# A deeper ring of exponential tiles, an earlier turn for the last shifted curves, and smaller filler matmuls in a multi-query attention kernel

## The chip, the cores and the metric

The kernel runs on one core of a Trainium2 chip. The metric is the device time of one execution in microseconds (us). A profiled execution has a span, from its first to its last instruction, that is about 2 us shorter than its device time (773.3 against 775.11 us for the kernel before). PE is TensorE, ACT is ScalarE, DVE is VectorE.

## The reference

The program takes x of 2048 rows by 512 in bf16 and returns `x + s * g`.

```python
xn = layernorm(x)
q  = (xn @ wq)            # 32 heads of 16
k  = xn @ wk              # one key head, 16 wide, shared by all heads
v  = xn @ wv              # one value head
p  = softmax(q k^T / 4)   # 32 heads x 2048 x 2048
s  = (p v) @ wo
g  = silu(silu(xn @ w1) @ w2)     # 1792 wide inside
return x + s * g
```

The work is 32 x 2048 x 2048 exponentials. The kernel cuts them into 2048 *score tiles* of 128 keys by 512 queries; 64 of them form a *group*, and there are 32 groups.

## The kernel before

The kernel is a list scheduler that runs when the program is built. It keeps a clock for every engine, knows an estimated duration of each operation, and writes down a fixed order of instructions for each engine. So a change of one of its constants changes the order of thousands of instructions; on the chip only the semaphores decide when each starts.

A score tile can go two ways. On ACT, two or three tiles that lie side by side in PSUM go through one exponential into a slot of the ring `pa_sb`. On DVE, one instruction turns a tile into a first curve (`db_sb`, a bf16 exponential built by integer arithmetic), and four tiles share four instructions that make *shifted curves* from it (`ds_sb`), whose weighted sum approximates the exponential. Either way PE then multiplies the curves by the values ("PV") and accumulates into one PSUM bank. That bank must be transposed out by DVE before the next group's PV may begin.

```python
NPA, NDB, NDS = 6, 4, 2 * (K - 1)          # six slots of exponentials
pa_sb = sb("pa_sb", [P, NPA, 3 * NQ], BF16)

def pv_round(t):                            # which PV matmuls can go now?
    # ... cut: nothing before the last group's bank is transposed
    if len(got) < 4 and nleft[g] > 0 and t - old < HOLD and a_pressure() < NPA - 2 and pe_share(t) > LOW_USE:
        return ("wait", min(soon, old + HOLD))
    return ("go", got)

def act_step():                             # ACT takes an exponential only with a free slot
    # ... cut
    free = [k for k in range(NPA) if pa_busy[k] == 0]
    if free:
        s = min(free, key=lambda k: pl.ready(AC, (), [("pA", k)]))
        rx = pl.ready(AC, [("ps", b) for b in u.banks[:len(u.slots)]], [("pA", s)])

# DVE: shifted curves have priority 6, evacuations of score tiles 0 or 2
pl.add(Task(DV, T_SH, lambda v, s=s, j=j, bb=bt.b: v.tensor_scalar(
    ds_sb[:, s, :], db_sb[:, bb, :], SHIFT[j], None, op0=ALU.add),
    [("Db", bt.b, i) for i in range(4)], ds_keys(s), 6, list(bt.P.values()), on_place=placed))

# a filler: four matmuls on zeros, when PE was busy less than LOW_USE of the last 3 us
elif st["assigned"] > 0 and not tail["made"]:
    fb = fill_bank(t)
```

The softmax here doesn't subtract the row's maximum and nothing guards it: scores larger than these inputs give would overflow.

## Time and profile before

The median is 773.68 us of 4 runs (772.73 to 774.03).

These are lines of the profile's page of the kernel before: busy time of each engine with its share of the span, the chain of waits by engine and by line, and the three costliest groups of ACT and DVE (after the bar: busy us, mean ns of one, then idle time just before them and what ended it).

```profile
PE 704.9 (91%) x8640; PEld 202.7 (26%) x8640; DVE 738.3 (95%) x1290; ACT 747.4 (97%) x758; POOL 19.9 (3%) x46
...
ACT 88%; DVE 6%; PE 5%; DMA 1%; issue 0%; SPq 0%; ACTq 0%; DVEq 0%
...
L1200 ACT ACTIVATE pa_sb<-ps 128x1024 bf16<-128x1024 f32 (+1 forms) x679 | 734.0, 1377 | 8.3 <-PE ps L695 4.7
L871 DVE TENSOR_SCALAR db_sb<-ps 128x512 uint16<-128x512 f32 x492 | 328.5, 686 | 13.8 <-PE ps L695 11.8
L905 DVE TENSOR_SCALAR ds_sb<-db_sb 128x2048 uint16<-128x2048 uint16 x492 | 323.6, 684 | 1.0
```

ACT is the bound: 88% of the chain, with 679 exponentials of 2 or 3 tiles. DVE makes 492 of the 2048 tiles. Mean durations overlap from one instruction to the next; in the chain of waits five exponentials in a row, three of two tiles and two of three (from 75.80 us), take 5.44 us. That is 12 tiles, so ACT needs about 0.453 us a tile.

The next answer cuts the span of the kernel before at the first exponential (13.62 us), at 22 us and at the end of the last exponential (763.83 us). Columns: stretch, its length, then busy us (and instructions) of PE, weight loads, DVE, ACT, POOL, the granted PE clock, the DMA share and GB/s.

```profile
core 0: us, PE busy (x) PEld busy (x) DVE busy (x) ACT busy (x) POOL busy (x), PEclk, DMA share, GB/s
0.00:13.62 13.62, 9.75 (x91) 4.22 (x92) 10.27 (x30) 3.94 (x7) 7.36 (x17) 1.00 0.86 280
13.62:22.00 8.38, 7.73 (x73) 3.40 (x71) 6.56 (x21) 6.18 (x5) 4.45 (x9) 0.59 1.08 375
22.00:763.83 741.83, 683.54 (x8416) 193.13 (x8414) 715.54 (x1229) 737.32 (x746) 8.14 (x20) 1.00 0.02 7
763.83:773.30 9.47, 3.85 (x66) 1.90 (x66) 5.93 (x12) 0.00 (x1) 0.00 (x0) 0.96 0.16 57
```

ACT idles 2.2 us in the head (8.38 less 6.18), while the clock of PE is granted at 0.59 on average, and 4.5 us in the body. The list of waits of the kernel before (us in total, times, longest) says for what, from 40 us on:

```profile
ACT pa_sb L1200 <- PE ps L965: 3.1, 3, 1.4
ACT pa_sb L1200 <- PE ps L695: 0.8, 1, 0.8
```

Line 965 is the PV matmul. An exponential reads scores, not PV, so a wait for PV is a wait for a free slot of the ring. The timeline of the kernel before shows the last of the three (start, duration, idle before it in brackets):

```profile
722.47 0.71 DVE L982 STREAM_TRANSPOSE f_sb<-ps 128x512 f32<-128x512 f32 x1
...
723.66 0.59 PE L965 MATMUL ps<-pa_sb,v_sb 128*32 128x512 bf16 x5
...
724.09 1.45 ACT L1200 ACTIVATE pa_sb<-ps 128x1536 bf16<-128x1536 f32 x1 [1.30 <-PE ps L965]
```

DVE transposes the output bank of a closing group at 722.47 us. Only then can PE consume exponentials of the next group (723.66 us), which empties a slot; ACT has stood for 1.30 us. DVE itself waits for score matmuls, 28 times from 40 to 757 us:

```profile
DVE db_sb L871 <- PE ps L695: 10.4, 28, 0.8
```

### The profile page before, as it was taken

To read this page: it belongs to the slowest core of one execution; us is meant where nothing else is said; L and a number is where in the kernel's file an instruction comes from. 1 tells how busy PE (TensorE), PEld (TensorE's weight loads), DVE (VectorE), ACT (ScalarE), POOL (GpSimd) and SP (SyncE) were. 2 spreads that over 40 slices of the span, in tenths; PEclk is the share of its full clock that TensorE was granted. 3 is DMA by queue.
4 is the path that set the end of the run, shared out by engine and by line. 5 is a ranking of instruction groups with operands and counts; after the bars stand their busy time and mean duration, and the time that the engine had idled before them with its cause. 6 is when DMAs were issued, how large, how long until landed. Compare 5 with 4: busy or idle time off the path is not lost.

```text
span 773.3 us, 19855 instructions
## 1 busy us (share of the span) xinstructions
PE 704.9 (91%) x8640; PEld 202.7 (26%) x8640; DVE 738.3 (95%) x1290; ACT 747.4 (97%) x758; POOL 19.9 (3%) x46
## 2 busy tenths in 40 slices
PE   7999899999989999999988999999998999999985
PEld 3322222222222222222222222222222222222221
DVE  8699999999999998999999999999999999999994
ACT  4999999999999999999999999999999999999995
POOL 5400000000000000000000000000000000000000
PEclk8999999999999999999999999999999999999999
DMA  9300000000000000000000100000000000000000
GB/s 311 85 3 2 2 1 2 2 2 2 1 2 16 29 14 2 2 2 1 2 2 2 29 28 2 2 1 2 3 2 1 15 16 29 2 3 1 2 2 28
DMA packets 11429, 12.57 MB, mean 16 GB/s; under 512 B 1808, under 2 KB 10768, under 8 KB 11344
## 3 DMA queue, kind: packets, MB, share of 16 engines
q1 hardware_dynamic: 10288, 11.28, 4.5%
q8 instruction: 69, 1.13, 0.6%
q10 hardware_dynamic: 1056, 0.03, 0.1%
q14 instruction: 16, 0.13, 0.1%
HBM read 8.95 MB, written 2.10 MB: 14 GB/s over the span
## 4 chain that ended last, share of the span: by engine, by line
ACT 88%; DVE 6%; PE 5%; DMA 1%; issue 0%; SPq 0%; ACTq 0%; DVEq 0%
ACT pa_sb L1200 83%; ACT t_sb L523 3%; DVE db_sb L871 2%; DVE ds_sb L905 2%; PE ps L965 1%; PE ps L695 1%; PE ps L396 1%; ACT t_sb L546 1%; DMA ds_sb<-in_A_x_dram 1%; DVE stats_sb L357 1%; PE ps L438 0%; SPq L315 0%; PE ps L412 0%; DVE f_sb L982 0%; DVE qt_sb L503 0%
## 5 line engine op out<-in xcount | busy, mean ns | idle before, releaser
L1200 ACT ACTIVATE pa_sb<-ps 128x1024 bf16<-128x1024 f32 (+1 forms) x679 | 734.0, 1377 | 8.3 <-PE ps L695 4.7
L871 DVE TENSOR_SCALAR db_sb<-ps 128x512 uint16<-128x512 f32 x492 | 328.5, 686 | 13.8 <-PE ps L695 11.8
L905 DVE TENSOR_SCALAR ds_sb<-db_sb 128x2048 uint16<-128x2048 uint16 x492 | 323.6, 684 | 1.0
L695 PE MATMUL ps<-qt_sb,kt_sb 32*128 32x512 bf16 x2048 | 267.7, 385 | 51.9 <-ACT pa_sb L1200 41.1
L965 PE MATMUL ps<-ds_sb,v_sb 128*32 128x512 bf16 x1968 | 258.5, 384 | 2.3 <-DVE ds_sb L905 1.7
L965 PE MATMUL ps<-pa_sb,v_sb 128*32 128x512 bf16 x1556 | 245.7, 386 | 2.3 <-DVE ds_sb L905 1.5
L695 PEld LDWEIGHTS ps<-qt_sb,kt_sb 32*128 32x128 bf16 x2048 | 68.5, 91 | 333.6 <-ACT pa_sb L1200 273.3
L965 PE MATMUL ps<-db_sb,v_sb 128*32 128x512 bf16 x492 | 132.5, 387 | 3.0 <-DVE f_sb L982 2.8
L965 PEld LDWEIGHTS ps<-ds_sb,v_sb 128*32 128x32 bf16 x1968 | 65.8, 95 | 63.5 <-issue 28.3
L965 PEld LDWEIGHTS ps<-pa_sb,v_sb 128*32 128x32 bf16 x1556 | 61.3, 95 | 55.5 <-issue 34.9
L396 PE MATMUL ps<-w_sb,u_sb 128*32 128x512 bf16 x896 | 75.1, 384 | 0.0
L396 PE MATMUL ps<-xnT_sb,w_sb 128*32 128x512 bf16 x896 | 72.5, 384 | 0.7 <-DVE db_sb L871 0.4
L523 ACT ACTIVATE t_sb<-ps 128x512 bf16<-128x512 f32 x56 | 47.5, 848 | 0.0
L965 PEld LDWEIGHTS ps<-db_sb,v_sb 128*32 128x32 bf16 x492 | 33.0, 95 | 21.8 <-issue 9.1
L525 DVE SCALAR_TENSOR_TENSOR u_sb<-t_sb,ps 128x512 bf16<-128x512 bf16 x56 | 38.2, 682 | 0.3 <-ACT t_sb L523 0.2
L982 DVE STREAM_TRANSPOSE f_sb<-ps 128x512 f32<-128x512 f32 x32 | 22.8, 712 | 7.4 <-PE ps L965 7.4
L396 PEld LDWEIGHTS ps<-w_sb,u_sb 128*32 128x32 bf16 x896 | 18.8, 94 | 29.9 <-issue 24.2
L396 PEld LDWEIGHTS ps<-xnT_sb,w_sb 128*32 128x32 bf16 x896 | 18.5, 94 | 29.5 <-issue 18.6
L396 PE MATMUL ps<-xnT_sb,wq_sb 128*32 128x512 bf16 x256 | 20.3, 383 | 0.0
L396 PE MATMUL ps<-wo_sb,on_sb 128*32 128x512 bf16 x256 | 19.9, 383 | 0.0
L986 DVE TENSOR_TENSOR otr_sb<-f_sb,rcp_sb 128x256 bf16<-128x256 f32 x32 | 13.3, 416 | 0.0
L546 ACT ACTIVATE t_sb<-ps 128x512 bf16<-128x512 f32 x16 | 13.0, 815 | 0.0
(44 smaller groups left out, 161.0 us busy)
## 6 DMA issues: line engine op xcount, KB each, us to landing
w_sb<-in_B_w_dram SPq DMA_DIRECT2D x2, 1792.0 KB, 13.2
xr_sb<-in_A_x_dram SPq DMA_DIRECT2D x16, 128.0 KB, 2.2
out_dram<-ob_sb SPq DMA_DIRECT2D x16, 128.0 KB, 1.7
ds_sb<-in_A_x_dram SPq DMA_DIRECT2D x3, 512.0 KB, 7.7
ds_sb<-in_A_x_dram SPq DMA_DIRECT2D x4, 128.0 KB, 2.6
wq_sb<-in_A_wq_dram SPq DMA_DIRECT2D x1, 512.0 KB, 5.4
wo_sb<-in_A_wo_dram SPq DMA_DIRECT2D x1, 512.0 KB, 14.6
kt_sb<-kt_sb SPq DMA_DIRECT2D x4, 64.0 KB, 2.3
```

What stands on the lines that cost most here:

```text
L357: ts_ = pl.add(Task(DV, 593.0, lambda v, t=t: v.bn_stats(stats_sb[:, t, :], x_tile(t)), [xkey(t)], [("st", t)], 1 + j, gate=(lambda: q_don ...
L396: last = h.matmul(bank(b)[32 * j:32 * (j + 1), :], lhsT=lhs(j), rhs=rhs, start=start, stop=stop, tile_position=(0, 32 * j), skip_group_che ...
L523: t1 = Task(AC, 477.0, lambda a: a.activation(t_sb[:, k, :], bank(b), ACT.Tanh, scale=0.5), [("ps", b)], [("t", k)], 0)
L525: t2 = Task(DV, T_P, lambda v: v.scalar_tensor_tensor(out=u_sb[:, ft, :], in0=t_sb[:, k, :], scalar=1.0, in1=bank(b), op0=ALU.add, op1=ALU ...
L546: t1 = Task(AC, 477.0, lambda a: a.activation(t_sb[:, k, :], bank(b), ACT.Tanh, scale=0.25), [("ps", b)], [("t", k)], 0)
L695: return pe.matmul(bank(b), lhsT=kt_sb[32 * i:32 * i + 32, g % 2, kt * P:(kt + 1) * P], rhs=qt_sb[32 * i:32 * i + 32, (g // 2) % NQR, :], ...
L871: bt.P[i] = pl.add(Task(DV, T_P, lambda v, b=b, i=i, bb=bt.b: v.tensor_scalar(db_sb[:, bb, i * NQ:(i + 1) * NQ], bank(b), 128.0 * LOG2E, 1 ...
L905: pl.add(Task(DV, T_SH, lambda v, s=s, j=j, bb=bt.b: v.tensor_scalar(ds_sb[:, s, :], db_sb[:, bb, :], SHIFT[j], None, op0=ALU.add), [("Db" ...
L965: h = pe.matmul(bank(OB)[32 * i:32 * (i + 1), :], lhsT=lhs, rhs=rhs, start=s0, stop=s1, tile_position=(0, 32 * i), skip_group_check=True)
L982: t1 = pl.add(Task(DV, T_TR, lambda v: v.transpose(f_sb[:, k, :], bank(OB)), [("ps", OB)], [("F", k)], 1, [norm.get(("m", g - 2))]))
L986: t3 = pl.add(Task(DV, 332.0, lambda v: v.tensor_tensor(o3[:, :, val:val + DH], f3[:, :, val:val + DH], rcp_sb[:, k, :].unsqueeze(2).to_br ...
L1200: op = pl.place(AC, 0.8333 * NQ * n + T_AF, lambda a: a.activation(pa_sb[:, s, 0:n * NQ], ps[:, b0 * 512:(b0 + n) * 512], ACT.Exp), [("ps" ...
```

## The change

Its intent: let ACT run ahead over the close of a group, close groups sooner, and keep PE's clock up with fillers that cost less.

```diff
-LOW_USE, USE_WIN = 0.5, 3000.0
+LOW_USE, HIGH_USE, USE_WIN = 0.55, 0.8, 3000.0
+CLOSING, URGENT = 3, 1.5
+NPA, PRESS = 9, 4
@@ pv_round and pe_step: the pressure threshold stays at four
-... a_pressure() < NPA - 2 and pe_share(t) > LOW_USE:
+... a_pressure() < PRESS and pe_share(t) > LOW_USE:
@@ shifted curves
-    ..., 6, list(bt.P.values()), on_place=placed))
+    ..., lambda g=bt.g: URGENT if g == st["gO"] and nleft[g] <= CLOSING else 6, list(bt.P.values()), on_place=placed))
@@ fillers
-if "zer" not in pl.lastw or pe_share(t) > LOW_USE:
+if "zer" not in pl.lastw or pe_share(t) > (LOW_USE if t > 30000.0 else HIGH_USE):
@@ do_fill: 256 columns instead of 512; one 128x128 matmul where PE is in that mode
-elif st["assigned"] > 0 and not tail["made"]:
+elif t_done and not tail["made"]:
     fb = fill_bank(t)
@@ cut: filler durations, warm-up condition
```

More of the change, by code (lines that the diff above doesn't have):

```diff
@@ L160, in best @@
             if r <= t + 25.0:
-                key = (task.prio, k)
+                key = (task.prio() if callable(task.prio) else task.prio, k)
                 if now is None or key < now[0]:
@@ L257, in bass_recurrent_scan__grouped_kv_mqa__dense_activation_silu__prompt_kernel @@
     POOL_BANKS = (5, 7)
-    NPA, NDB, NDS = 6, 4, 2 * (K - 1)
+    NDB, NDS = 4, 2 * (K - 1)
     NQR, NON = 4, 2 * NOC
@@ L392, in job, with col4 @@
             return jb
-        def col4(h, b, lhs, rhs, start, stop):
+        def col4(h, b, lhs, rhs, start, stop, n=NQ):
             for j in range(4):
-                last = h.matmul(bank(b)[32 * j:32 * (j + 1), :], lhsT=lhs(j), rhs=rhs, start=start, stop=stop,
+                last = h.matmul(bank(b)[32 * j:32 * (j + 1), 0:n], lhsT=lhs(j), rhs=rhs, start=start, stop=stop,
                                 tile_position=(0, 32 * j), skip_group_check=True)
@@ L906, in make_shifts @@
                         ds_sb[:, s, :], db_sb[:, bb, :], SHIFT[j], None, op0=ALU.add),
-                        [("Db", bt.b, i) for i in range(4)], ds_keys(s), 6, list(bt.P.values()), on_place=placed))
+                        [("Db", bt.b, i) for i in range(4)], ds_keys(s),
+                                lambda g=bt.g: URGENT if g == st["gO"] and nleft[g] <= CLOSING else 6, list(bt.P.values()), on_place=placed))
         x_free = [False]
@@ L938, in pv_round @@
                 return ("wait", soon)
-            if len(got) < 4 and nleft[g] > 0 and t - old < HOLD and a_pressure() < NPA - 2 and pe_share(t) > LOW_USE:
+            if len(got) < 4 and nleft[g] > 0 and t - old < HOLD and a_pressure() < PRESS and pe_share(t) > LOW_USE:
                 return ("wait", min(soon, old + HOLD))
@@ L1118, in do_fill @@
         def do_fill(t, b):
-            pl.place(PE, MM, lambda pe: col4(pe, b, lambda j: zer_sb[:, 32 * j:32 * (j + 1)], zer_sb[:, :], True, True),
-                     ["zer"], [("ps", b)], t0=pe_start(t, "C"))
-            pl.mode = "C"
+            mode = pl.mode if pl.mode in ("C", "F") else "C"
+            if mode == "C":
+                emit = lambda pe: col4(pe, b, lambda j: zer_sb[:, 32 * j:32 * (j + 1)], zer_sb[:, 0:NQ // 2], True, True, NQ // 2)
+            else:
+                emit = lambda pe: pe.matmul(bank(b)[:, 0:NQ // 2], lhsT=zer_sb[:, 0:P], rhs=zer_sb[:, 0:NQ // 2], start=True, stop=True)
+            pl.place(PE, MM / 2, emit, ["zer"], [("ps", b)], t0=pe_start(t, mode))
+            pl.mode = mode
             st["fills"] = st.get("fills", 0) + 1
@@ L1134, in pe_step @@
             col = None
-            if pr and pr[0] == "go" and (a_pressure() >= NPA - 2):
+            if pr and pr[0] == "go" and (a_pressure() >= PRESS):
                 col = ("pv", pr[1])
@@ L1151, in pe_step @@
                 elif col is not None:
-                    mode = col[1].mode if col[0] == "job" else "C"
-                    dur = col[1].rounds[col[1].pos][2] if col[0] == "job" else MM
+                    mode = col[1].mode if col[0] == "job" else pl.mode if col[0] == "fill" and pl.mode == "F" else "C"
+                    dur = col[1].rounds[col[1].pos][2] if col[0] == "job" else MM / 2 if col[0] == "fill" else MM
                     end = pe_start(t, mode) + dur + SWITCH
@@ L1172, in pe_step @@
                     nxt = min(nxt, c)
-            if st["assigned"] < 3 and "zer" in pl.lastw and pl.ready(PE, ["zer"], [("ps", 7)]) <= t and (
-                    not t_done or INF > nxt > t + 230.0) and 7 in pool_free:
+            if not t_done and "zer" in pl.lastw and pl.ready(PE, ["zer"], [("ps", 7)]) <= t:
                 n = st["warm"] = st.get("warm", 0) + 1
@@ L1193, in act_step @@
                     rx = pl.ready(AC, [("ps", b) for b in u.banks[:len(u.slots)]], [("pA", s)])
-            if now is not None and (rx is None or now[2] <= max(t, rx) or now[1].prio < 0):
+            if now is not None and (rx is None or now[2] <= max(t, rx) or False):
                 pl.place_task(now[1])
```

## The prediction

> **What bounds the kernel now.** The table of engines: ACT 747.4 us of 773.3 (97%), DVE 738.3 (95%), PE 704.9 (91%). The chain of waits is 88% ACT, 83% the exponential on line 1200. Two engines share 2048 score tiles: ACT exponentiates 1556, DVE makes 492 (lines 871 and 905). In the chain of waits six two-tile exps take 5.44 us, so ACT needs 0.454 us a tile; a DVE step there takes 0.60 us, so a DVE tile needs 1.20 us. Together 2.20 + 0.83 = 3.03 tiles/us (estimates). A microsecond of ACT idleness removed is thus worth about 0.73 us of span, one of DVE idleness 0.27 us, if the new order gives the freed engine more tiles.
>
> **What idleness there is.** The table of windows shows ACT full from 22 to 763 us but near 516, 584 and 723 us. The list of waits agrees: after 40 us ACT waits 3.1 us for PV matmuls (three times: no free slot in the ring) and 0.8 us for score matmuls, all close to the end of a group, where PV of the next group queues until the output bank is transposed. At 512 us PE idled, and the granted clock fell to 0.5 for about 3.5 us. In the head ACT stalls 0.81, 0.49 and 0.99 us between its first exps (17.3 to 22.1 us), with the clock at 0.5 from about 14.7 to 21 us. The Trainium skill, "TensorE: Matmul & The Clock Gate" (Part 1: The HAM clock gate), describes this halving after an idle window; this trace agrees. DVE waits 10.4 us for score matmuls in 28 pieces between 40 and 757 us, and about 5 us between 28 and 38 us, before all keys are projected. From last exp to end is an untouched tail of 9.5 us.
>
> **What the change does.** Only fillers are added or removed.
> - Ring of nine: removes the 3.1 us of ACT waits on PV: 3.1 x 0.73 = 2.3 us.
> - Shifted curves first at a close: groups close one or two DVE steps (0.6 to 1.2 us) earlier, but evacuations wait as long. I expect 4 to 5 of DVE's 10.4 us to go, x 0.27 = 1.2 us.
> - Fillers among the first projections: full clock from 14 to 21 us. 1.5 of ACT's 2.3 us of stalls go (1.1 us); keys come about 2 us earlier, so DVE starts its tiles earlier (0.5 us). Fillers delay first projections by some tenths (-0.4 us).
> - Half-size fillers: before has 11 rounds of four, 4.8 us of PE in all, mostly slack. Fewer dips of the clock: 0.6 us.
>
> Sum 5.3 us: 768.5 us. 2% would be 15.5 us; all idleness of ACT and DVE in the body is worth less than 10 us. PE at 91% has little slack, so a reshuffled order can lose by chance.
>
> **Prediction:** 768.5 us, 8 in 10 within 763.5 to 773.0. Faster by over 2%: 0.03; within 2%: 0.95; slower by over 2%: 0.02.
>
> **What would show it.** ACT's wait on line 965 gone; granted clock 1.0 from 14 to 22 us and near 513 us; ACT unbroken from before 20 us; DVE's wait for score matmuls after 40 us below 7 us; last exp about 5 us earlier, the same 9.5 us tail.
>
> **What would make it wrong.** PE, not the ring, then holds ACT (waits on line 695); delayed evacuations hold up score banks; fillers push the first exp beyond 13.6 us; or a new dip of the clock where the order changed.

## The result

The changed kernel takes 770.33 us (median of 4 runs, 769.54 to 770.64), the kernel before 773.68 us. A ratio is the mean time of one kernel's fast runs over that of the other's fast runs of the same rounds, so it is not quite the ratio of the medians; here it is 0.9957 (0.994 to 0.9974). On another chip the changed kernel took 769.59 us against 773.6, ratio 0.9946. So the gain is 3.4 to 4.0 us, inside the range predicted and less than the 5.3 us forecast.

The lines of the page of the changed kernel that answer to those above (line numbers moved by a few: 1206 is the exponential, 697 the score matmul, 968 the PV matmul):

```profile
PE 708.2 (92%) x8669; PEld 201.6 (26%) x8669; DVE 738.2 (96%) x1290; ACT 748.2 (97%) x773; POOL 20.0 (3%) x46
...
ACT 95%; DVE 1%; PE 1%; DMA 1%; issue 0%; SPq 0%; DVEq 0%
...
L1206 ACT ACTIVATE pa_sb<-ps 128x1024 bf16<-128x1024 f32 (+1 forms) x694 | 737.2, 1391 | 2.8 <-PE ps L697 2.7
L873 DVE TENSOR_SCALAR db_sb<-ps 128x512 uint16<-128x512 f32 x492 | 327.0, 685 | 11.2 <-PE ps L697 9.4
L907 DVE TENSOR_SCALAR ds_sb<-db_sb 128x2048 uint16<-128x2048 uint16 x492 | 321.7, 684 | 0.9
```

And the span of the changed kernel, cut at its first exponential (13.78 us), at 22 us and at the end of its last exponential (759.29 us), columns as before:

```profile
core 0: us, PE busy (x) PEld busy (x) DVE busy (x) ACT busy (x) POOL busy (x), PEclk, DMA share, GB/s
0.00:13.78 13.78, 10.77 (x97) 4.95 (x97) 10.30 (x30) 3.94 (x8) 7.37 (x17) 1.00 0.91 287
13.78:22.00 8.22, 7.37 (x88) 3.25 (x90) 7.32 (x23) 7.06 (x6) 4.47 (x9) 0.79 1.08 367
22.00:759.29 737.29, 686.68 (x8440) 191.79 (x8438) 714.63 (x1227) 737.21 (x761) 8.17 (x20) 1.00 0.02 7
759.29:768.80 9.51, 3.38 (x57) 1.62 (x50) 5.93 (x12) 0.00 (x0) 0.00 (x0) 0.92 0.16 55
```

Nearly the whole difference is in the middle two rows. From first to last exponential it is 750.2 us before and 745.5 us after. ACT's idle time there falls from 6.7 us (2.2 + 4.5) to 1.24 us (1.16 + 0.08), and its work grows by 0.8 us (743.50 to 744.27): there are 15 exponentials more, because more of them take two tiles instead of three. The tail after the last exponential is 9.5 us in both. In the body ACT now has no idle time to speak of; the list of waits has no line for ACT after 40 us. DVE's wait for score matmuls fell too, but only to this:

```profile
DVE db_sb L873 <- PE ps L697: 7.9, 24, 0.9
```

Two things deserve notice. DVE still makes exactly 492 tiles, so ACT still makes 1556. And the clock in the head was still halved, though for a shorter time. The spans differ by 4.5 us, more than the medians: the profiled run of the kernel before was one of its slower ones (775.11 us, 1.4 us above the median). So the waits listed for it are those of one slow run, and not to be leaned on to a microsecond.

### The profile page after: what moved, and what is told of

It reads as the page before. It is cut to its first block, busy times and chain, and to the rows that moved or that the text cites. A ratio compares the mean times of both kernels' runs of the same rounds, so it can differ in the third digit from the quotient of the medians.

```text
span 768.8 us, 19950 instructions
## 1 busy us (share of the span) xinstructions
PE 708.2 (92%) x8669; PEld 201.6 (26%) x8669; DVE 738.2 (96%) x1290; ACT 748.2 (97%) x773; POOL 20.0 (3%) x46
## 4 chain that ended last, share of the span: by engine, by line
ACT 95%; DVE 1%; PE 1%; DMA 1%; issue 0%; SPq 0%; DVEq 0%
ACT pa_sb L1206 91%; ACT t_sb L525 4%; ACT t_sb L548 1%; DMA ds_sb<-in_A_x_dram 1%; DVE stats_sb L359 1%; PE ps L697 0%; PE ps L440 0%; SPq L317 0%; PE ps L398 0%; PE ps L968 0%; PE ps L414 0%; DVE xnT_sb L425 0%; DVE f_sb L985 0%; DVE ob_sb L565 0%; DVE on_sb L996 0%
## 5 line engine op out<-in xcount | busy, mean ns | idle before, releaser
L697 PE MATMUL ps<-qt_sb,kt_sb 32*128 32x512 bf16 x2048 | 272.9, 384 | 47.7 <-ACT pa_sb L1206 35.9
L968 PE MATMUL ps<-pa_sb,v_sb 128*32 128x512 bf16 x1556 | 257.5, 385 | 0.8 <-ACT pa_sb L1206 0.4
L968 PEld LDWEIGHTS ps<-pa_sb,v_sb 128*32 128x32 bf16 x1556 | 63.6, 94 | 52.5 <-issue 34.1
L398 PE MATMUL ps<-xnT_sb,w_sb 128*32 128x512 bf16 x896 | 76.6, 385 | 0.6 <-DVE u_sb L527 0.4
L525 ACT ACTIVATE t_sb<-ps 128x512 bf16<-128x512 f32 x56 | 48.8, 872 | 0.0
L968 PEld LDWEIGHTS ps<-db_sb,v_sb 128*32 128x32 bf16 x492 | 33.0, 94 | 20.4 <-issue 10.4
L548 ACT ACTIVATE t_sb<-ps 128x512 bf16<-128x512 f32 x16 | 13.8, 860 | 0.0
```

What stands on the lines that cost most here:

```text
L398: last = h.matmul(bank(b)[32 * j:32 * (j + 1), 0:n], lhsT=lhs(j), rhs=rhs, start=start, stop=stop, tile_position=(0, 32 * j), skip_group_c ...
L525: t1 = Task(AC, 477.0, lambda a: a.activation(t_sb[:, k, :], bank(b), ACT.Tanh, scale=0.5), [("ps", b)], [("t", k)], 0)
L548: t1 = Task(AC, 477.0, lambda a: a.activation(t_sb[:, k, :], bank(b), ACT.Tanh, scale=0.25), [("ps", b)], [("t", k)], 0)
L697: return pe.matmul(bank(b), lhsT=kt_sb[32 * i:32 * i + 32, g % 2, kt * P:(kt + 1) * P], rhs=qt_sb[32 * i:32 * i + 32, (g // 2) % NQR, :], ...
L968: h = pe.matmul(bank(OB)[32 * i:32 * (i + 1), :], lhsT=lhs, rhs=rhs, start=s0, stop=s1, tile_position=(0, 32 * i), skip_group_check=True)
```

## The experiments

All twelve kernels gave a correct result, and 5 rounds were asked for each. In three expectations (of the ring alone, the fillers alone, and the ring with the moved constant) the counted DVE tiles are one too many, because a lone one-tile exponential was taken for a DVE tile; the traces have 492, 500 and 488, and one exponential more.

### The ring alone

```diff
 (kernel before)
-NPA = 6          # threshold NPA - 2 = 4
+NPA, PRESS = 9, 4
```

> The kernel before with nothing changed but the ring, nine exp tiles deep (the pressure threshold stays at four). The build gives 682 exponentials and 493 DVE tiles. Theory A (the ring is the whole gain, as ACT's waits on PV were ring waits): 3.4 us below before, or more, near 769.5 us; ACT's wait on PV gone from the list of waits. Theory B (three parts, each a share, as predicted: ring 2.3, closing 1.2, fillers 1.8 us): 771.4 us.

Measured: 770.16 us against 773.54 us for the kernel before on the same chip, ratio 0.9952 (0.9938 to 0.9965). That is 3.7 us, as much as the whole change gives (3.4 and 4.0 us). ACT has no wait after 40 us. Theory A holds and theory B, my prediction's split, falls, if narrowly: 2.3 us would be a ratio of 0.9970, just outside the interval. The ring removes ACT's 3.1 us of waits for PV, and also the 0.8 us wait for score matmuls at 516 us. In the profile of the kernel before, that one lies in a stretch of halved clock (513 to 516 us) that follows PE's idling at the close of a group; that the shallow ring caused it is argued, not shown. The page of the ring-only kernel has no wait of the exponentials for PV left:

```profile
L1202 ACT ACTIVATE pa_sb<-ps 128x1024 bf16<-128x1024 f32 (+2 forms) x683 | 735.9, 1406 | 1.4 <-PE ps L697 1.2
```

Nine slots give the chip more room and also change the planned order; the two were not separated.

### The priority at the close alone, and the fillers' part alone

```diff
 (kernel before)
-    ds_keys(s), 6,
+    ds_keys(s), lambda g=bt.g: 1.5 if g == st["gO"] and nleft[g] <= 3 else 6,
```

> The kernel before with nothing but the priority of shifted curves of a closing group. Theory A: within 0.7 us of before, ACT's waits on PV still there. Theory B: 1.2 us below before, and DVE's wait for score matmuls after 40 us well under 10.4 us.

Measured: 773.03 us, ratio 0.9997 (0.9985 to 1.001). ACT waits 1.5 us for PV, DVE 8.1 us for score matmuls (40 to 757 us). The shorter waits for PV fit groups that close sooner, and DVE does lose 2.3 of its 10.4 us of waits; but DVE makes 492 tiles as before, and the time stays.

```diff
 (kernel before)
-LOW_USE = 0.5
+LOW_USE, HIGH_USE = 0.55, 0.8      # and 256-column fillers, and fillers after the first transposes
```

> The kernel before with nothing but the fillers' part (half size, thresholds 0.55 and 0.8, fillers between the first projections). With a ring of six this reshuffles the order: 501 DVE tiles and 673 exponentials instead of 492 and 679. Theory A: no gain, 773 to 776 us, ACT's waits on PV as large as before or larger. Theory B: 1.8 us below before.

Measured: 773.27 us, ratio 0.9992 (0.9978 to 1.0005), inside theory A's range. The lines of ACT from the list of waits of this kernel, from 40 us on (967 is the PV matmul here):

```profile
ACT pa_sb L1205 <- PE ps L967: 6.7, 7, 2.0
ACT t_sb L548 <- PE ps L398: 0.3, 1, 0.3
```

This order gives DVE 8 tiles more, so ACT has 8 x 0.454 = 3.6 us less to do. But ACT's waits for the ring grew by 3.6 us, from 3.1 to 6.7. The two cancel: in this order, what DVE takes off ACT is lost again in ring waits.

### The whole change with the ring put back to six

```diff
 (changed kernel)
-NPA, PRESS = 9, 4
+NPA, PRESS = 6, 4
```

> The changed kernel with the ring put back to six. Theory A: the gain goes, 773 us or above. Theory B: 2.3 us above the changed kernel, 772.6 us. A third theory C (closing and fillers relieve the ring of six by themselves, so ring and the other two replace each other): 770 to 772 us although the ring is six.

Measured: 771.03 us, ratio 0.9968 (0.9955 to 0.9982), so 2.5 us below before, and no ring waits. Theory A is wrong about this kernel, and theory C is right: the closing priority and the fillers, which do nothing each by itself, together spare this order the ring waits. In the orders run here they and the ring replace each other; they do not add. Whether the pair does this for any order, or whether this order is a lucky one, is left open. The next pair shows how much a neighbouring order can cost with six slots.

### An unrelated constant moved by 5%, with six slots and with nine

```diff
 (kernel before; then the same with nine slots)
-DVE_LIMIT = 4000.0
+DVE_LIMIT = 3800.0
```

The constant limits the work queued for DVE. It has no part in the change, but it does bear on the split of the tiles.

> The kernel before with one unrelated constant of its scheduler moved by 5% (limit of queued DVE work 3800 instead of 4000), ring of six. It gives another order: 500 DVE tiles, 676 exponentials. Theory L (a ring of six makes the time depend on the luck of the order, and the kernel before was tuned to a lucky one): ACT waits over 8 us on PV, 776 to 781 us. Rival (orders are worth the same within noise): 772.5 to 774.5 us.

> The same moved constant (3800) with the ring nine deep: 489 DVE tiles, 689 exponentials. Theory L: no wait on PV, and within 2.5 us of the ring-only kernel with 4000, so 770 to 772.7 us. Rival: the same as the ring-of-six kernel with 3800, less some 3.5 us.

Measured with six slots: 776.77 us against 772.69 us for the kernel before, ratio 1.0053 (1.0041 to 1.0065). With nine: 772.31 us, ratio 0.9992 (0.9979 to 1.0005). The list of waits of the six-slot kernel after 40 us:

```profile
ACT pa_sb L1202 <- PE ps L967: 9.6, 9, 2.1
ACT t_sb L525 <- PE ps L398: 0.2, 1, 0.2
```

Theory L holds with six slots: this order waits 9.6 us for the ring, so the constants of the kernel before stood at a better place than this neighbour. With nine it holds in part: no wait for PV and a time within 770 to 772.7 us, but by the ratios 3.1 us above the ring-only kernel, not within 2.5. At the moved constant the ring is worth 0.0061 x 772.7 = 4.7 us, at the old one 3.7 us; with some 1.4 us of uncertainty on the first (from the two intervals) these are not clear of each other, and the rival of 3.5 us is not excluded. Nine slots do not make orders equal: this one gives DVE only 488 tiles and is about 3 us slower than the ring-only kernel (0.9992 against 0.9952), of which the 4 tiles for ACT explain 1.8 us.

### Fillers put into the head's real gap

The changed kernel places its new fillers too early. Its timeline of PE in the head (start, duration, instructions; idle time in brackets), with 1126 the fillers, 440 and 398 the first projections, 697 the first scores:

```profile
8.67 1.15 PE L1126 MATMUL ps<-zer_sb 128*128 128x256 bf16 x9
9.75 0.41 PE L440 MATMUL ps<-xnT_sb,wke_sb 128*32 128x128 bf16 x16
9.98 1.04 PE L398 MATMUL ps<-xnT_sb,wq_sb 128*32 128x512 bf16 x16
10.84 0.82 PE L440 MATMUL ps<-xnT_sb,wke_sb 128*32 128x384 bf16 x16
13.34 0.39 PE L697 MATMUL ps<-qt_sb,kt_sb 32*128 32x512 bf16 x3 [1.67 <-DVE qt_sb L505]
```

The idle 1.67 us before the first scores got none: the scheduler was holding PE for the score matmuls there and does not ask for a filler in that branch. So one batch was forced in, every other instruction keeping its place.

```diff
 (changed kernel, the branch that reserves PE for the next scores)
     if max(ts, end) > max(ts, act_need() - 446.0) + S_TOL:
+        if t < 16000.0 and ts - t > 400.0 and 7 in pool_free and ...:
+            pl.place(PE, 250.0, gap, ["zer"], [("ps", 7)], t0=t)    # ten half-size matmuls
         pl.clk[PE] = ts
         return True
```

> The changed kernel with ten half-size filler matmuls put where none was placed: after the first key projection, in PE's idle time just before the first score matmuls (11.6 to 13.3 us in the changed trace). Every other instruction keeps its place. Theory H (the halved clock after that gap costs ACT its head stalls): granted clock 1.0 from 14 to 22 us, ACT's two stalls of 0.48 and 0.47 us gone, 0.7 to 1.2 us below the changed kernel, near 769.4 us. Rival (the stalls come from the order of first projections, whatever the clock): within 0.4 us of the changed kernel.

> The changed kernel with the ten fillers before the first score matmuls, once more, now beside the changed kernel. Theory H: the head's clock stays full, and the median is 0.5 to 1.2 us below the changed kernel's of this call. Rival: the gain seen in the one profile is a matter of where the clock's windows fall in a run; medians within 0.4 us.

> The changed kernel, unaltered, on the same chip as the other three, for a direct comparison. 0.4 to 0.5% below before, about 769.5 to 770.5 us.

The fillers land where they should, in the timeline of the first of these kernels:

```profile
11.24 0.82 PE L440 MATMUL ps<-xnT_sb,wke_sb 128*32 128x384 bf16 x16
12.00 1.27 PE L1168 MATMUL ps<-zer_sb 128*128 128x256 bf16 x10
13.20 0.39 PE L697 MATMUL ps<-qt_sb,kt_sb 32*128 32x512 bf16 x3
```

Measured: 769.8 us the first time (ratio to before 0.9966, 0.9951 to 0.9982); the second time, beside the changed kernel, 769.15 us against 769.59 us (ratios 0.9945 and 0.9946). In both profiles, and in that of the last experiment, the granted clock is 1.00 from 14 to 24 us. Three lines for that stretch, columns as before: the changed kernel, the first kernel with these fillers, and the version of 764.67 us (told next) without them.

```profile
14.00:24.00 10.00, 9.15 (x106) 4.15 (x105) 9.10 (x31) 8.84 (x8) 5.05 (x11) 0.83 0.99 334
14.00:24.00 10.00, 8.45 (x115) 4.13 (x117) 9.56 (x29) 9.91 (x9) 5.54 (x14) 1.00 1.00 336
14.00:24.00 10.00, 7.93 (x103) 3.79 (x103) 9.46 (x29) 9.04 (x9) 5.49 (x14) 1.00 0.99 336
```

Of the eleven profiles without these fillers three have a full clock there too, and eight do not: the changed kernel had 0.83 in each of its two profiles, the kernel before 0.66. The three full ones have the same order of PE's first 150 matmuls as the kernel before: one order, and a clock that is full in some profiles and not in others. The Trainium skill, "TensorE: Matmul & The Clock Gate" (Part 1: The HAM clock gate), says that the window of activity is free-running and does not start with the kernel; that fits a head whose clock differs from run to run, and the halved stretches here last 3.4 us (16.4 to 19.8 us, changed kernel) or twice that (14.7 to 21.5 us, before).

So what theory H says of the clock is supported and not shown: with the fillers it is full in both profiles of the changed kernel, without them in none of the four that have its PE order in the head; the third profile with fillers proves nothing, as that version had a full clock without them. About the time it is not shown either: 0.4 us between medians and equal ratios are no verdict, and the means of the five runs each differ by 0.1 us, with an uncertainty of about 1 us (my estimate from their spread). In the second of these profiles stalls of 0.38 and 0.26 us after the first run of exponentials remain with the clock full.

### More tiles for DVE, with nine slots and with six

With the ring deep enough, DVE's idle time is what is left. The limits on DVE's queued work were loosened on the ring-only kernel; the values were picked among some hundred sets of constants for an order with more DVE tiles and little planned idle time, and this one order was run.

```diff
 (ring-only kernel)
-DVE_LIMIT, TWO_LIMIT, PRESS = 4000.0, 1500.0, 4
+DVE_LIMIT, TWO_LIMIT, PRESS = 5500.0, 2000.0, 5
```

> The kernel before with ring nine, pressure threshold five, limit of queued DVE work 5500, two-tile limit 2000; no closing priority, no filler change. The order has 500 DVE tiles and 670 exponentials against 492 and 694 of the changed kernel. Theory S (after the ring, the split of tiles is what is left, for DVE stays idle for 9 us and more): ACT has 8 tiles less (8 x 0.454 = 3.6 us) and 24 instructions less, so 4 to 5 us below the changed kernel, 765.5 to 767 us, DVE's wait for score matmuls after 40 us under 3 us. Rival P (PE at 92% gives no more): ACT waits on score matmuls in the body instead, 769 us or above.

Measured: 764.67 us against 772.69 us, ratio 0.9904 (0.9889 to 0.9919). DVE makes 500 tiles and waits 2.2 us for score matmuls (40 to 757 us), ACT waits for nothing after 40 us. Between this and the ring-only kernel lie 0.0048 of 773 us, 3.7 us; 8 tiles less for ACT are worth 3.6 us. Theory S holds (the time is even below its 765.5 to 767 us, on a chip where the kernel before is about 0.9 us faster than on the others), and PE at 92% was no obstacle. This version beats both kernels. Its exponentials on the page:

```profile
L1202 ACT ACTIVATE pa_sb<-ps 128x1024 bf16<-128x1024 f32 (+1 forms) x670 | 730.7, 1412 | 1.5 <-PE ps L697 1.4
```

```diff
 (the version just told)
-NPA, PRESS = 9, 5
+NPA, PRESS = 6, 4
```

> The best version so far with the ring back at six and the pressure threshold at four as before; the limits of 5500 and 2000 stay. The order has 504 DVE tiles and 677 exponentials. Theory S (the ring is what lets the other limits be loosened, since a DVE with more queued work closes groups later and PV waits longer): ACT waits 8 us or more on PV and the time is 773 to 777 us although ACT has 12 tiles less than in the changed kernel. Rival (the limits alone make the best version): 766 to 769 us.

Measured: 773.51 us against 773.6 us, ratio 1.0004 (0.999 to 1.0018). In an answer for 40 to 750 us of this kernel DVE is busy for 705.47 of 710 us, more than in any other, and ACT for only 700.87. The list of waits after 40 us:

```profile
ACT t_sb L525 <- PE ps L398: 4.9, 3, 3.1
ACT pa_sb L1202 <- PE ps L967: 2.9, 4, 1.2
ACT pa_sb L1202 <- PE ps L697: 0.7, 2, 0.5
ACT t_sb L548 <- PE ps L398: 0.3, 1, 0.3
```

Theory S predicted the time but put the waits in the wrong place: 2.9 us are for PV, not 8. The larger part, 4.9 us, is before the tanh of the dense branch. That the scheduler put tanh there because no slot was free is my reading of the code, not shown. The sum is 9 us of idle ACT all the same, and all 12 tiles taken off ACT bring nothing.

```diff
 (the version with 764.67 us)
+ the ten fillers before the first scores
```

> The best version so far with the ten fillers before the first score matmuls. Its profile already had a full clock there once. Theory H: 0.3 to 1 us below the best version, 763.7 to 764.4 us. Rival: 764.5 to 765.5 us.

Measured: 765.22 us against 773.6 us, ratio 0.9894 (0.9879 to 0.9908), against 0.9904 without the fillers on another chip. The intervals overlap, so this is inconclusive: the time lies in the rival's range, the ratio 0.8 us lower, and the clock in the head was full without the fillers too.

Busy time of ACT from 40 to 750 us in one profile each, taken from 710, gives ACT's idle time in the body:

| kernel | slots | DVE tiles | exponentials | ACT idle, us | ratio to before |
|---|---|---|---|---|---|
| before | 6 | 492 | 679 | 4.34 | 1 |
| closing priority alone | 6 | 492 | 694 | 2.62 | 0.9997 |
| fillers' part alone | 6 | 500 | 674 | 7.19 | 0.9992 |
| before, constant moved | 6 | 500 | 676 | 10.20 | 1.0053 |
| best limits, six slots | 6 | 504 | 677 | 9.13 | 1.0004 |
| change with six slots | 6 | 492 | 694 | 0.40 | 0.9968 |
| ring alone | 9 | 492 | 683 | 0.00 | 0.9952 |
| whole change | 9 | 492 | 694 | 0.00 | 0.9957, 0.9946 |
| ring, constant moved | 9 | 488 | 690 | 0.67 | 0.9992 |
| best limits | 9 | 500 | 670 | 0.00 | 0.9904 |

Every order with nine slots keeps ACT full, but for 0.67 us in one. With six, the orders that give DVE more tiles have the most idle time on ACT. Which is the cause is not shown. With the constant moved, six slots gave DVE 500 tiles and nine 488; with the best limits 504 and 500. So it may also be that an ACT held up by the ring in the plan leaves tiles to DVE.

## Why the prediction was right or wrong

- **The total** was right within its range: 770.33 and 769.59 us for 768.5, within 2%. That was partly luck: the ring's term was 1.4 us too small, the other three together 3.0 us too large, and the errors partly cancelled. The range also reached up to 773.0 us, nearly no gain at all.
- **The ring's mechanism** was right: the three waits on PV were ring waits and are gone. Its size was wrong. The step that failed is "A microsecond of ACT idleness removed is thus worth about 0.73 us of span, ... if the new order gives the freed engine more tiles". The new order gave neither engine more tiles (492 before and after), so by the same reasoning the worth of ACT's idle time is 1 and not 0.73, and that of DVE's 0 and not 0.27. The term of 2.3 us measures 3.7 us alone (2.7 to 4.8 by its interval), for the 3.9 us of waits after 40 us. That fits a worth of 1, but the interval alone does not exclude 0.73 x 3.9 = 2.8 us; the unmoved split is what speaks against it.
- **The closing priority**, 1.2 us, failed at the same step: DVE's wait fell from 10.4 to 8.1 us (I expected 4 to 5 us to go), and none of it became time: 0.9997.
- **The fillers in the head**, 1.1 + 0.5 - 0.4 us, failed at "full clock from 14 to 21 us": the clock was halved in both profiles of the changed kernel, whose scheduler put no filler into the 1.67 us gap. With fillers there the clock was full in both profiles, and even then no gain clear of noise was seen (0.4 us between medians).
- **The half-size fillers**, 0.6 us: the fillers' part alone measures 0.9992, not clear of nothing; a new order with longer ring waits ate what its 8 tiles were worth. Fewer dips of the clock are likely, not shown: from 40 to 750 us none of the six profiles with half-size fillers has a halved stretch, and four of the other eight have one of 3.4 us each (at 513 us in the kernel before).
- **The sum of shares was wrong in kind.** I added four gains. The ring alone gives all, and the other two parts give 2.5 us only when the ring is six: in the orders run here they are substitutes.
- **Of what was to be seen**, ACT's wait on PV is gone, the tail is unchanged at 9.5 us and the last exponential ends 4.5 us earlier. DVE's wait stayed at 7.9 us instead of below 7, and ACT ran nearly unbroken only from 21 us on, not from before 20.

## What to carry to other kernels

Before pricing idle time on two engines that share a pool of work, look whether the split of the pool will move; with a fixed split, only the idle time of the engine that ends last is worth anything. When a fixed order is tuned around a small buffer, deepen the buffer first and then retune: here three slots gave 3.7 us, and looser limits, which gave nothing with six slots, 3.7 us more. And test a scheduling change against a neighbouring order, since a 5% move of a constant outside the change cost as much as the whole change gained.

## What the Trainium skill lacked or had wrong

- "TensorE: Matmul & The Clock Gate", Part 1 (HAM oscillation), gives as the rule that PE should have no idle gaps above about 3.4 us. Here the clock was halved at 14.71 us (kernel before) though the longest gap before it was 1.67 us; in the 3.41 us up to then the profile has PE busy for 1.50 us. In the changed kernel it was halved at 16.40 us, after 3.41 us with PE busy for 2.41 us. A rule on gaps alone does not cover this. The same page (A second HAM failure mode) does tell of a clock that oscillates when PE idles briefly and often, but gives no length for such idles.
- "ScalarE: Activation LUTs" (What ACT_TABLE_LOAD costs) gives 186 ns + 0.833 ns per column for an activation with immediate scale and bias, and an overlap of about 93 ns back to back; as an estimate from that page, a 1024-column exponential would cost 946 ns in a run. Here one costs about 0.91 us in a run (the chain has pieces of 5.44 and 6.35 us that differ by one two-tile exponential), while a lone one takes 1.02 us, so the overlap here is nearer 0.11 us.
- "TensorE: Matmul & The Clock Gate", Part 1, says that the warm-up differs from run to run, and puts its penalty under 1% of a typical span; no page that I used gives the spread of whole runs. The 31 runs of the kernel before, taken beside the experiments, range from 771.48 to 775.35 us at mean granted clocks of 0.993 to 0.999, the slowest at 0.993; at 0.997 alone they range from 771.48 to 774.08 us, so the clock is not the whole of it. A change of under 1 us needs many rounds here.
